# A linear-attention and dense-layer kernel: stores and loads of values issued from ScalarE's queue

## The chip, the cores and the metric

The kernel runs on one core of a Trainium2 chip. Times are device microseconds of that core for one execution. Five engines work side by side, each through its own list of instructions in order: TensorE (PE; its weight loads are shown as PEld), VectorE (DVE), ScalarE (ACT), GpSimd (POOL) and SyncE (SP). SP computes nothing; it issues transfers. A transfer (DMA) is issued by an instruction of one engine and then carried out by the core's 16 DMA engines; other engines learn through a semaphore that it has landed.

## The reference

The program computes gated linear attention and feeds its result to a dense layer. For each of 4 × 8 heads a 48 × 48 state decays row by row and takes in one key-value product per token; the output token is the query times the state:

```python
state = alpha[:, :, t, :, None] * state + np.einsum('bhd,bhe->bhde', k[:, :, t], v[:, :, t])
y[:, :, t] = np.einsum('bhd,bhde->bhe', q[:, :, t], state)
```

The 768 tokens of each of 4 batches, 384 wide, then go through two matrix products with a squared relu between them:

```python
h = x @ w_in                  # 3072 x 384 by 384 x 2048
r = np.maximum(h, 0.0)
g = r * r
return (g @ w_out)            # by 2048 x 384
```

Inputs and output are float32; the kernel multiplies in bfloat16.

## The kernel before

The work is cut into 12 units of 256 tokens (4 batches by 3 stretches of the sequence, batches running fastest). Each unit passes through these steps:

- Four loads bring alpha, k, q and v of the unit into one of four float32 buffers called raw (names lda, ldk, ldq, ldv with the unit's number; line 456). Unit g uses buffer g mod 4, so a load waits until unit g − 4 is done with that quarter of the buffer.
- The front turns alpha into logarithms (ACT), sums them over tokens with a triangular matrix (PE) and takes exponentials (ACT), which scale k and q (DVE) into a bfloat16 tile qks. v is cast to bfloat16 (vbf, names vc, mostly on POOL, L631).
- From unit 3 on, qks is transposed by DMA into kqt (names tr0 and tr1, L652), two transfers per unit issued by SP. Before that PE does it.
- The scores are multiplied on PE (psX and psZ, L838), masked on DVE (pm, L849), and with vbf and the carried state give the attention output in psX (L724 to L771), which ACT copies to xbf (names xe, L894).
- x is transposed to xt, from unit 4 on by a DMA that SP issues (L915), before that by PE (L909).
- The first layer (names s1, L965) makes 8 blocks per unit in two PSUM banks that alternate. Each block is relued into rr by ACT (re, L973) or DVE (L975) and squared into gt by ACT (sq, L987) or DVE (L983).
- The second layer (names s2, L1005) sums 16 products in psO for each half of the tokens; the result is copied to the output buffer osb by ACT (oe, L1012) or DVE (L1014), and for units 0 to 10 one store of 384 KB writes both halves to HBM (names out0_1 to out10_1, L1023). There are two buffers osb, so the evictions of unit g wait for the store of unit g − 2. The last unit has three smaller stores (L1016 and L943).

The loads of units 1 and 2 and the weights w_in and w_out are issued by POOL; all other transfers by SP.

The order in which each engine does its operations is written out by hand in a table of names, one list per engine (TABLES, L203). `schedule` takes the lists as they are; `place` then puts a semaphore wait ahead of an operation wherever something it needs runs on another engine or is a transfer and isn't known to be done through earlier waits of the same engine. Each engine works through its list in order, so an operation that waits holds back all that stand behind it.

What decides the engine for a transfer is the first argument of `add` in `load` (L458) and in `second_layer` (the call of `add` behind `store`, L1022), together with the list in which the name stands. A transfer's semaphore is named after what it moves and the engine that issues it.

Of the kernel before, what the change touches and what calls it, by code (L numbers as in the profile page):

```python
# [24 lines left out]
class Program:  # L25
# [13 lines left out]
    def add(self, eng, fn, cost, prio, reads=(), writes=(), name="", dma=None, lag=0, after=(), mode=("F", "F"),  # L39
            alts=None):  # L40

        reads, writes = ([h for k in keys for h in ((k + (0,), k + (1,)) if len(k) == self.HALVED.get(k[0]) else (k,))]
                         for keys in (reads, writes))
        choices = {eng: (fn, cost)}
        if alts:
            choices.update(alts)
        op = Op(choices, prio, name)
        op.idx = len(self.ops)
        op.lag = lag
        op.mode = mode  # L50
        if dma is not None:
            op.sem = (dma, 0)
        for o in after:
            op.deps[o] = True
        for k in reads:
            w = self.writer.get(k)
            if w is not None:
                op.deps[w] = True
            if k[0] == "ps":
                for r in self.readers.get(k, ()):  # L60
                    op.deps.setdefault(r, False)
        for k in writes:
            w = self.writer.get(k)
            if w is not None:
                op.deps[w] = True
            for r in self.readers.get(k, ()):
                if r is not op:
                    op.deps.setdefault(r, False)
        for k in reads:
            self.readers.setdefault(k, []).append(op)  # L70
        for k in writes:
            self.writer[k] = op
            self.readers[k] = []
        op.deps.pop(op, None)
        self.ops.append(op)
        return op
# [93 lines left out]
    def emit(self):  # L170
# [54 lines left out]
    "act": """  # L225
        table copycaus ln0_0 ln1_0 ei0_0 ea0_0 ei1_0 ea1_0 ec0_0 ec1_0 et00_0 et10_0 vc0 ln1 vc1 ei1 ea1 xe0 ec1 xv0
        re0_0 re0_1 sq0_1 re0_2 re0_3 ln2 xe1 ei2 ea2 re0_6 ec2 re0_7 es2 re1_0 re1_1 sq0_5 re1_3 et1_2 sq1_1 sq1_3
        oe0_0 ln3 ei3 ea3 re1_7 ec3 sq1_5 ln4 es3 re1_6 xe2 ei4 ea4 lm4 oe1_0 re2_1 ec4 re2_0 ln5 es4 re2_2 ei5
        re2_3 re2_4 lm5 ea5 ec5 re2_5 sq2_1 sq2_5 oe1_1 xe3 ln6 re2_6 sq2_7 sq2_6 es5 re3_1 re3_0 ei6 ea6 re3_3 ec6
        re3_2 oe2_0 re3_5 ln7 lm6 re3_4 sq3_5 xe4 re3_6 sq3_7 ei7 es6 ea7 oe3_0 re4_1 xe5 ec7 lm7 re4_2 sq4_3 re4_4  # L230
        re4_5 sq4_5 oe3_1 re4_7 ln8 es7 ei8 re5_2 oe4_0 lm8 re5_3 ea8 re5_4 re5_5 xe6 oe4_1 es8 re5_7 sq5_7 sq5_6
        re6_0 re6_1 re6_2 re6_3 re6_4 ln9 re6_5 xe7 ei9 ea9 lm9 oe5_1 sq6_5 es9 re6_6 re6_7 sq6_6 sq6_7 re7_0 re7_1
        sq7_1 re7_3 lm10 ln10 sq7_3 re7_4 ei10 ea10 re7_6 lm11 es10 sq7_6 sq7_7 ln11 re8_0 ei11 re8_2 vc10 ea11
        re8_4 xe9 re8_5 oe7_1 sq8_7 re9_1 re9_0 sq9_1 re9_3 re9_2 sq9_3 xe10 es11 oe8_1 re9_7 sq9_7 re10_1 re10_0
        sq10_1 re10_2 re10_5 sq10_3 sq10_5 re10_6 sq10_7 re11_1 re11_0 oe10_0 re11_3 re11_2 sq11_3 re11_4 re11_5
        oe10_1 re11_6 re11_7 oe11_0 oe11_10
    """,
    "dve": """
        zzero zlinc zlstr zident zcaus zcaus1 zones zown zlaf0 own0 zlaf1 own1 zqks0 zqks1 zqks2 zlab0 zlab1 ekm0_0
# [13 lines left out]
        vc4 bk5 pr7 vc5 vc6 vc7 pr8 vc8 pr9 vc9 pr10 pr11 vc11  # L253
    """,
    "sp": """
        lda0 ldk0 ldq0 ldv0 lda3 ldv3 ldk3 lda4 ldq3 ldq4 ldk4 lda5 ldv4 tr1_3 tr0_3 lda6 ldq5 tr1_4 ldk5 tr0_4
        out0_1 lda7 ldv5 ldk6 tr1_5 tr0_5 ldv6 xt4 out1_1 ldq6 ldk7 ldq7 ldv7 xt5 lda8 tr1_6 tr0_6 out2_1 ldk8 ldq8
        tr1_7 tr0_7 xt6 ldv8 lda9 out3_1 tr1_8 tr0_8 ldq9 xt7 ldv9 ldk9 lda10 out4_1 lda11 tr1_9 xt8 ldk10 ldq10
        out5_1 tr0_9 ldv10 ldv11 tr0_10 tr1_10 xt9 ldk11 ldq11 out6_1 out7_1 xt10 tr0_11 tr1_11 out8_1 xt11 out9_1
        out10_1 out11_0 out11_10 out11_11  # L260
    """,
}

# [1 line left out]
def pe_ns(count, cols, at_once=1):  # L265
    return count * max(cols / 2.4 + 2.5, 25) / at_once


def act_ns(n):
    return 180 + n * 0.8333  # L270


def dve_ns(n, rate=1.0):
    return 150 + n / 0.96 / rate
# [6 lines left out]
def bass_gla_recurrent__then__act_relu_squared_kernel(  # L281
# [25 lines left out]
    POOL_LOADS = (1, 2)  # L307
# [56 lines left out]
    add = pr.add  # L364
# [25 lines left out]
    for buf, key, val in ((LINC[:], "linc", 1.0), (LSTR[:], "lstr", 1.0), (IDENT[:], "ident", 0.0),  # L390
# [3 lines left out]
        name="slinc")  # L394
    add("pool", select(LSTR[:], ALU.is_gt, 0.0, 0, [[1, 128]], -1), 300, -1e6, reads=[("lstr",)], writes=[("lstr",)],
        name="slstr")
# [7 lines left out]
    for c, key in enumerate(("caus", "caus1")):  # L404
        add("pool", select(flat[c], ALU.is_ge, 0.0, 128 * c, [[-1, 2], [1, 2], [2, 64]], -2), 400, -1e6 + 7,
            reads=[(key,)], writes=[(key,)], name=f"s{key}")
    add("act", lambda e: e.activation(flat[1][0:64], flat[0][0:64], AF.Copy), 400, -1e6 + 8,
        reads=[("caus",), ("caus1",)], writes=[("caus1",)], name="copycaus")
# [6 lines left out]
    def piece(fj):  # L415
        return max(w for w, (at, n) in enumerate(PIECES) if at <= fj)
# [24 lines left out]
    def load(g):  # L441
        b, i = units[g]
        t0 = i * T
        p0 = g * P
        r, la, qs, kt, pm, vb, x2 = (g % n for n in (NRAW, 2, NQKS, NKQT, NPM, NV, 2))
        first, last = i == 0, i == NST - 1
        sr, sw = 2 * b + i % 2, 2 * b + (i + 1) % 2

        for j, t, nm in ((0, alpha, "a"), (1, k, "k"), (2, q, "q"), (3, v, "v")):
            src = t[b, :, t0:t0 + T, :].rearrange("h (p j) d -> p h (j d)", j=2)  # L450
            dst, key = RAW[r][:, j].rearrange("p h j d -> p h (j d)"), ("raw", r, j)
            gate = AFTER.get((g, nm), AFTER.get(g))
            parts = ((0, slice(0, 4)), (1, slice(4, 8))) if (g, nm) in HALF_LOADS else (("", slice(0, 8)),)
            for x, hs in parts:
                def run(e, dst=dst[:, hs], src=src[:, hs]):
                    return e.dma_start(dst, src)  # L456

                ring = "pool" if g in POOL_LOADS else "sp"  # L458
                load_op[g, nm] = add(ring, run, 930 if ring == "pool" else 600, L_PRIO[g] + j, writes=[key if x == "" else key + (x,)],
                                     name=f"ld{nm}{g}{x}", dma=f"{nm}{r}{x}", after=[load_op[gate]] if gate else [])  # L460

# [527 lines left out]
    def second_layer(g):  # L989
        b, i = units[g]  # L990
        gt = g % NGT
        p0 = DENSE.get(g, g * P + 20500)
        ob = g % NOSB
        for j in range(2):
            rows = slice(b * S + i * T + j, b * S + i * T + T, 2)
            if g == G - 1 and j == 1:
                last_tile(gt, rows, p0 + P)
                continue
            psS, keyS = (psX[:, 0, 0:DM], ("ps", "X", 0)) if (g, j) in IN_X else (psO[:, 0:DM], ("ps", "O"))
            for sg in range(4):  # L1000
                ps_ = p0 + P * 0.5 + 600 + (j * 4 + sg) * P * 0.5 / 8

                def s2(pe, sg=sg, j=j, psS=psS):
                    for fj in range(sg * FT // 4, (sg + 1) * FT // 4):
                        ins = pe.matmul(psS, GT[gt][:, fj, j, :], WOUT[:, fj, :],  # L1005
                                        start=(fj == 0), stop=(fj == FT - 1))
                    return ins

                add("pe", s2, pe_ns(FT // 4, DM), ps_,
                    reads=[("gt", gt, fj) for fj in range(sg * FT // 4, (sg + 1) * FT // 4)] + [("wout", piece(sg * FT // 4))],  # L1010
                    writes=[keyS], name=f"s2_{g}_{j}_{sg}")
            add("act", lambda e, j=j, psS=psS: e.activation(OSB[ob][:, j], psS, AF.Copy), act_ns(DM), ps_ + 700,  # L1012
                reads=[keyS], writes=[("osb", ob, j)], name=f"oe{g}_{j}",
                alts={"dve": (lambda e, j=j, psS=psS: e.tensor_copy(OSB[ob][:, j], psS), dve_ns(DM))})  # L1014
            if g == G - 1:
                add("sp", lambda e, rows=rows: e.dma_start(out[rows, :], OSB[ob][:, 0]), 600, ps_ + 1300,  # L1016
                    reads=[("osb", ob, 0)], name=f"out{g}_0", dma=f"o{ob}", lag=600)
            elif j == 1:

                dst = out[b * S + i * T:b * S + i * T + T, :].rearrange("(p j) n -> p (j n)", j=2)  # L1020

                def store(e, dst=dst):  # L1022
                    return e.dma_start(dst, OSB[ob][:].rearrange("p j n -> p (j n)"))  # L1023

                add("sp", store, 600, ps_ + 1300, reads=[("osb", ob, 0), ("osb", ob, 1)], name=f"out{g}_1",
                    dma=f"o{ob}")

    L_PRIO = {g: (g - 4) * P for g in range(G)}
# [3 lines left out]
    for g in range(3, G):  # L1032
        ORDER += [f"f{g}", f"w{g - 1}", f"p{g}"]
    ORDER += [f"y{G - 1}"]
    AFTER = {1: (0, "a"), ("win", 0): (0, "k"), ("win", 1): (0, "k"), 2: ("win", 0), ("wout", 0): ("win", 1),
             ("wout", 1): (2, "k"), 3: ("wout", 0)}
    load(0)
    load(1)
    for w in range(len(PIECES)):
        weight(0, w)  # L1040
    load(2)
    for w in range(len(PIECES)):
        weight(1, w)
    for st in ORDER:
        kind, g = st[0], int(st[1:])
# [46 lines left out]
```

## Time and profile before

| what | value |
|---|---|
| median of 3 timed runs | 176.03 us (175.4 to 178.41) |
| profiled execution | 174.4 us |
| its span, first to last instruction | 172.7 us |
| PE busy | 167.6 us, 97% of the span |
| PEld, DVE, ACT, POOL busy | 130.4, 122.3, 113.7, 26.9 us |
| queue of SP's transfers | 69024 packets, 26.75 MB, 66.6% of the 16 engines' time |
| queue of POOL's transfers | 1984 packets, 6.29 MB, 15.3% |

All of these but the timed runs come from one execution that was recorded by the hardware profiler. Issuing a transfer isn't counted as busy time; such rows are shown as SPq, with the time that the issuing instruction took, not the transfer itself. In a timeline row stand the start in us from the span's start, the duration in us, engine, line, operation, output and input, the count of instructions merged, and in brackets how long the engine was idle before and what ended that. In the chain of work that ended last, a row gives start, duration, engine, output and line. In the list of waits a row gives the engine and the line that waited, what it waited for, the total in us, how many times and the longest.

### The profile page before, as it was taken

How to read it: one execution, taken by the hardware profiler on the slowest of the kernel's cores; microseconds unless marked ns; L12 is line 12 of the kernel's file. 1: busy time of each engine (PE TensorE's matmuls, PEld its weight loads, DVE VectorE, ACT ScalarE, POOL GpSimd, SP SyncE). 2: the span in 40 equal slices, each digit the busy share in tenths (PEclk: the TensorE clock that was granted, in tenths of full speed). 3: DMA queues.
4: the chain of work that ended last, by engine and by line, in shares of the span. 5: the costliest groups of instructions: out<-in, count | busy, mean ns of one | idle time of the engine just before them, and what ended most of it. 6: DMA issues, size and time to landing. Idle time of an engine off the chain costs nothing.

```text
span 172.7 us, 5090 instructions
## 1 busy us (share of the span) xinstructions
PE 167.6 (97%) x2232; PEld 130.4 (76%) x2234; DVE 122.3 (71%) x202; ACT 113.7 (66%) x201; POOL 26.9 (16%) x37
## 2 busy tenths in 40 slices
PE   7999999899999999999999999999999999999994
PEld 2656888577887877888777878887787977778773
DVE  5379599679967979999796839679768663762110
ACT  4757768659789974588466589767552946356740
POOL 4920750030120040105000401220010000000000
PEclk9999999999999999999999999999999999999999
DMA  5999999999999998999995979949949448022022
GB/s 145 351 292 212 270 233 172 283 286 297 204 213 191 232 257 168 273 243 188 255 165 128 285 149 245 270 90 286 277 66 238 174 77 181 4 53 87 0 93 91
DMA packets 71030, 33.36 MB, mean 193 GB/s; under 512 B 67552, under 2 KB 67808, under 8 KB 71008
## 3 DMA queue, kind: packets, MB, share of 16 engines
q1 hardware_dynamic: 69024, 26.75, 66.6%
q0 software_dynamic: 1984, 6.29, 15.3%
q8 instruction: 17, 0.28, 0.6%
q14 instruction: 5, 0.04, 0.1%
HBM read 25.17 MB, written 4.72 MB: 173 GB/s over the span
## 4 chain that ended last, share of the span: by engine, by line
PE 79%; DMA 16%; POOL 3%; issue 1%; DVE 0%
PE psO L1005 34%; PE psWH L965 33%; DMA wout<-in_moe_w_out_dram 5%; DMA win<-in_moe_w_in_dram 5%; DMA raw<-in_k_dram 3%; POOL raw L456 3%; PE psX L735 2%; PE psZ L703 2%; DMA raw<-in_alpha_dram 2%; PE psX L838 2%; PE psX L724 2%; PE psX L935 2%; PE psZ L838 1%; PE psWH L574 1%; PE psX L909 0%
## 5 line engine op out<-in xcount | busy, mean ns | idle before, releaser
L965 PE MATMUL psWH<-xt,win 128*128 128x256 bf16 x576 | 73.0, 274 | 0.0
L1005 PE MATMUL psO<-wout,gt 128*128 128x384 bf16 x368 | 68.2, 326 | 0.6 <-DMA wout<-in_moe_w_out_dram 0.6
L965 PEld LDWEIGHTS psWH<-xt,win 128*128 128x128 bf16 x576 | 65.2, 145 | 4.6 <-ACT xt L923 0.4
L973 ACT ACTIVATE rr<-psWH 128x512 bf16<-128x512 f32 x70 | 41.3, 595 | 21.9 <-PE psWH L965 20.8
L1005 PEld LDWEIGHTS psO<-wout,gt 128*128 128x128 bf16 x368 | 35.0, 98 | 19.0 <-DMA wout<-in_moe_w_out_dram 0.8
L987 ACT ACTIVATE gt<-rr 128x1024 bf16<-128x1024 bf16 (+1 forms) x31 | 26.9, 890 | 3.5 <-DVE rr L975 3.1
L975 DVE TENSOR_SCALAR rr<-psWH 128x512 bf16<-128x512 f32 x26 | 17.7, 688 | 10.0 <-PE psWH L965 9.7
L983 DVE TENSOR_TENSOR gt<-rr 128x1024 bf16<-128x1024 bf16 (+1 forms) x29 | 17.2, 597 | 9.6 <-ACT rr L973 9.4
L631 POOL CAST vbf<-raw 128x768 bf16<-128x768 f32 x9 | 8.1, 899 | 68.3 <-DMA raw<-in_v_dram 68.3
L849 DVE TENSOR_TENSOR pm<-psX,caus 128x1024 bf16<-128x1024 f32 x12 | 14.6, 1220 | 4.0 <-PE psZ L838 4.0
L849 DVE TENSOR_TENSOR pm<-psZ,caus 128x1024 bf16<-128x1024 f32 x12 | 14.6, 1219 | 3.4 <-PE psZ L838 3.4
L1012 ACT ACTIVATE osb<-psO 128x384 f32<-128x384 f32 x14 | 6.9, 491 | 10.1 <-PE psO L1005 8.8
L1061 PE MATMUL psO<-zero 128*128 128x512 bf16 (+1 forms) x32 | 9.9, 437 | 1.5 <-DVE zero L376 1.3
L894 ACT ACTIVATE xbf<-psX 128x768 bf16<-128x768 f32 x10 | 8.1, 808 | 4.5 <-PE psX L724 4.1
L636 DVE TENSOR_TENSOR qks<-raw,eq 128x384 bf16<-128x384 f32 x18 | 10.5, 587 | 0.4 <-ACT eq L611 0.3
L641 DVE TENSOR_TENSOR qks<-raw,ek 128x768 bf16<-128x768 f32 x11 | 10.5, 954 | 0.1
L585 ACT ACTIVATE ek<-psWH 128x384 f32<-128x384 f32 x10 | 4.9, 489 | 5.9 <-PE psWH L574 3.8
L567 POOL TENSOR_TENSOR prd<-raw 128x384 f32<-128x384 f32 x6 | 6.2, 1035 | 16.3 <-DMA raw<-in_alpha_dram 16.3
L1014 DVE COPY osb<-psO 128x384 f32<-128x384 f32 x9 | 5.0, 555 | 4.8 <-PE psO L1005 4.6
L594 DVE TENSOR_TENSOR ek<-ek,raw 128x384 f32<-128x384 f32 x9 | 5.0, 553 | 3.7 <-ACT ek L585 3.7
L568 ACT ACTIVATE lab<-prd 128x384 bf16<-128x384 f32 x10 | 5.2, 518 | 2.4 <-POOL prd L567 1.4
L1061 PEld LDWEIGHTS psO<-zero 128*128 128x128 bf16 x34 | 3.2, 109 | 4.5 <-issue 1.9
(116 smaller groups left out, 166.0 us busy)
## 6 DMA issues: line engine op xcount, KB each, us to landing
out_dram<-osb SPq DMA_DIRECT2D x11, 384.0 KB, 4.4
raw<-in_alpha_dram SPq DMA_DIRECT2D x10, 384.0 KB, 5.0
raw<-in_k_dram SPq DMA_DIRECT2D x10, 384.0 KB, 4.2
raw<-in_q_dram SPq DMA_DIRECT2D x10, 384.0 KB, 5.0
raw<-in_v_dram SPq DMA_DIRECT2D x10, 384.0 KB, 5.1
win<-in_moe_w_in_dram POOLq DMA_DIRECT2D x2, 768.0 KB, 10.3
wout<-in_moe_w_out_dram POOLq DMA_DIRECT2D x2, 768.0 KB, 8.6
raw<-in_alpha_dram POOLq DMA_DIRECT2D x2, 384.0 KB, 4.6
```

The lines of the kernel that those rows point to most:

```text
L631: add("pool", lambda e: e.tensor_copy(vout, vin), 830, p0 + 900, reads=[("raw", r, 3)], writes=[("vbf", vb)], name=f"vc{g}", alts={"act": ...
L636: add("dve", lambda e, j=j, dst=dst: e.tensor_tensor(dst, RAW[r][:, 2, :, j, :].rearrange("p (n x) d -> p n x d", x=2), EQ[la][:, j].rearr ...
L641: add("dve", lambda e, a=a, E=E: e.tensor_tensor(QKS[qs][:, a, :, :, 0:D], RAW[r][:, 1 + a].rearrange("p h j d -> p j h d"), E[la][:].rear ...
L849: add("dve", lambda e, hf=hf, psT=psT: e.tensor_tensor(PM[pm][:, hf].rearrange("p r n j t -> p (r n) (j t)"), psT[:, :, :].rearrange("p r ...
L894: add("act", lambda e: e.activation(XBF[x2][:], psX[:, :, 0:HD], AF.Copy), act_ns(2 * HD), p0 + 6100, reads=[("ps", "X", 0), ("ps", "X", 1 ...
L965: ins = pe.matmul(psH[hb][:, i * T:(i + 1) * T], WIN[:, kk, hidden(fj)], mov, start=(kk == 0), stop=(kk == KT - 1))
L973: add("act", lambda e, hb=hb, rr=rr: e.activation(rr, psH[hb], AF.Relu), act_ns(512), pu + 600, reads=[("ps", "H", hb)], writes=[("rr", rb ...
L975: alts={"dve": (lambda e, hb=hb, rr=rr: e.tensor_scalar(rr, psH[hb], 0.0, None, ALU.max), dve_ns(512))})
L983: add("dve", lambda e, dst=dst, sq=sq: e.tensor_tensor(dst, sq, sq, ALU.mult), 148 + k * 267, pu + 1200, reads=[("rr", rb, h) for h in ran ...
L987: "act": (lambda e, dst=dst, sq=sq: e.activation(dst, sq, AF.Square), act_ns(k * 512))})
L1005: ins = pe.matmul(psS, GT[gt][:, fj, j, :], WOUT[:, fj, :], start=(fj == 0), stop=(fj == FT - 1))
L1061: pr.schedule(TABLES, (zero, lambda n: lambda pe: pe.matmul(psO[:, 0:n], ZERO[:, 0:128], ZERO[:, 0:n], skip_group_check=True)))
```

## The change

The stores of units 0 to 10 and the loads of v of units 4 to 11, 19 transfers in all, are issued from ACT's list instead of SP's. In ACT's list each name is put between the operations beside which SP issued it; the order of all other names is as before, on every engine.

```diff
@@ ACT's list: names put in (the rest unchanged)
+ldv4 after ln4      out0_1 after re2_6    ldv5 after sq2_6
+ldv6 after sq3_5    out1_1 after sq3_7    ldv7 after ea7
+out2_1 after re4_7  ldv8 after es8        out3_1 after sq5_7
+ldv9 after lm9      out4_1 after es9      out5_1 after ea10
+ldv10 after sq7_6   ldv11 after re8_0     out6_1 after oe7_1
+out7_1 after sq8_7  out8_1 after sq9_7    out9_1 after re10_6
+out10_1 after oe10_1
@@ SP's list: the same 19 names taken out
@@ in load(g)
-                ring = "pool" if g in POOL_LOADS else "sp"
+                ring = "pool" if g in POOL_LOADS else "act" if nm in "v" and g >= 4 else "sp"
@@ in second_layer(g)
-                add("sp", store, 600, ps_ + 1300, reads=[("osb", ob, 0), ("osb", ob, 1)], name=f"out{g}_1",
+                add("act", store, 600, ps_ + 1300, reads=[("osb", ob, 0), ("osb", ob, 1)], name=f"out{g}_1",
                     dma=f"o{ob}")
```

The evictions that wait for a store (L1012 on ACT, L1014 on DVE) and the casts of v (L631) now wait on the semaphores of ACT's transfers. In ACT's list the stores of units 7 and 10 carry a wait for an eviction on ACT itself and the store of unit 9 one for an eviction on DVE; the other 16 moved transfers carry no wait of their own there. SP's end waits for the last stores of both engines.

More of the change, by code (lines that the diff above doesn't have):

```diff
@@ L227 @@
         re0_0 re0_1 sq0_1 re0_2 re0_3 ln2 xe1 ei2 ea2 re0_6 ec2 re0_7 es2 re1_0 re1_1 sq0_5 re1_3 et1_2 sq1_1 sq1_3
[L228 to L236, printed above, removed]
+        oe0_0 ln3 ei3 ea3 re1_7 ec3 sq1_5 ln4 ldv4 es3 re1_6 xe2 ei4 ea4 lm4 oe1_0 re2_1 ec4 re2_0 ln5 es4 re2_2 ei5
+        re2_3 re2_4 lm5 ea5 ec5 re2_5 sq2_1 sq2_5 oe1_1 xe3 ln6 re2_6 out0_1 sq2_7 sq2_6 ldv5 es5 re3_1 re3_0 ei6
+        ea6 re3_3 ec6 re3_2 oe2_0 re3_5 ln7 lm6 re3_4 sq3_5 ldv6 xe4 re3_6 sq3_7 out1_1 ei7 es6 ea7 ldv7 oe3_0 re4_1
+        xe5 ec7 lm7 re4_2 sq4_3 re4_4 re4_5 sq4_5 oe3_1 re4_7 out2_1 ln8 es7 ei8 re5_2 oe4_0 lm8 re5_3 ea8 re5_4
+        re5_5 xe6 oe4_1 es8 ldv8 re5_7 sq5_7 out3_1 sq5_6 re6_0 re6_1 re6_2 re6_3 re6_4 ln9 re6_5 xe7 ei9 ea9 lm9
+        ldv9 oe5_1 sq6_5 es9 out4_1 re6_6 re6_7 sq6_6 sq6_7 re7_0 re7_1 sq7_1 re7_3 lm10 ln10 sq7_3 re7_4 ei10 ea10
+        out5_1 re7_6 lm11 es10 sq7_6 ldv10 sq7_7 ln11 re8_0 ldv11 ei11 re8_2 vc10 ea11 re8_4 xe9 re8_5 oe7_1 out6_1
+        sq8_7 out7_1 re9_1 re9_0 sq9_1 re9_3 re9_2 sq9_3 xe10 es11 oe8_1 re9_7 sq9_7 out8_1 re10_1 re10_0 sq10_1
+        re10_2 re10_5 sq10_3 sq10_5 re10_6 out9_1 sq10_7 re11_1 re11_0 oe10_0 re11_3 re11_2 sq11_3 re11_4 re11_5
+        oe10_1 out10_1 re11_6 re11_7 oe11_0 oe11_10
     """,
@@ L255 @@
     "sp": """
[L256 to L260, printed above, removed]
+        lda0 ldk0 ldq0 ldv0 lda3 ldv3 ldk3 lda4 ldq3 ldq4 ldk4 lda5 tr1_3 tr0_3 lda6 ldq5 tr1_4 ldk5 tr0_4 lda7 ldk6
+        tr1_5 tr0_5 xt4 ldq6 ldk7 ldq7 xt5 lda8 tr1_6 tr0_6 ldk8 ldq8 tr1_7 tr0_7 xt6 lda9 tr1_8 tr0_8 ldq9 xt7 ldk9
+        lda10 lda11 tr1_9 xt8 ldk10 ldq10 tr0_9 tr0_10 tr1_10 xt9 ldk11 ldq11 xt10 tr0_11 tr1_11 xt11 out11_0
+        out11_10 out11_11
     """,
```

## The prediction

> **What bounds the kernel now.** I read the page's shares first, then the busy time by stretch, then who waits for whom from 33.2 us to the end, and last the timelines of SP, ScalarE (ACT) and the chain.
>
> ```profile
> PE 167.6 (97%) x2232; PEld 130.4 (76%) x2234; DVE 122.3 (71%) x202; ACT 113.7 (66%) x201; POOL 26.9 (16%) x37
> 33.22:54.60 21.38, 21.38 (x305) 16.50 (x306) 17.94 (x31) 16.10 (x33) 3.48 (x4) 1.00 1.05 243
> 54.60:80.00 25.40, 25.40 (x369) 20.30 (x367) 22.53 (x35) 18.77 (x36) 4.20 (x4) 1.00 1.06 235
> 80.00:105.00 25.00, 25.00 (x375) 19.80 (x372) 18.63 (x29) 16.05 (x30) 2.94 (x3) 1.00 0.88 187
> 105.00:130.00 25.00, 25.00 (x317) 20.32 (x314) 19.42 (x29) 17.08 (x31) 3.67 (x4) 1.00 0.92 211
> 130.00:155.00 25.00, 24.93 (x334) 19.81 (x332) 16.20 (x25) 13.68 (x20) 0.00 (x0) 1.00 0.48 119
> PE psO L1005 <- DMA wout<-in_moe_w_out_dram: 0.6, 1, 0.6
> ACT rr L973 <- PE psWH L965: 19.5, 28, 1.6
> ACT osb L1012 <- PE psO L1005: 8.8, 7, 2.2
> ```
>
> A stretch's row gives its length, then busy time of PE, PEld, DVE, ACT and POOL; the last three numbers are granted clock, DMA share and GB/s. Over the five stretches from 33.22 to 155 us PE is busy 121.71 of 121.78 us, at clock 1.00. After 33.2 us the only wait that PE shows is 0.6 us for a weight load. So TensorE sets the end, and no transfer that SP issues is late for it: what SP is relieved of buys at most 0.07 us in these stretches. ACT works 81.7 of the same 121.78 us, and its largest idle times end with a PE result (19.5 and 8.8 us). That idle time is the cover under which ACT can take new work. The question is only whether it lies where the new work is put.
>
> **What is moved and what it costs.** The first moved transfer stands behind the logarithm of unit 4, at 40 us; the head up to 33.22 us is untouched. Nineteen DMA issues go to ACT: 11 stores and 8 loads of values. Each stands in ACT's order where ACT was when SP issued it. The same bytes start within about a microsecond of where they started, and the 26 transposes and the loads of alpha, k and q on SP stand where they stood, with gaps closed up.
>
> The price of one issue on ACT is on no row. The nearest rows are the same instructions on SP:
>
> ```profile
> 40.46 1.16 SPq L456 DMA_DIRECT2D raw<-in_v_dram  x1
> 52.81 2.41 SPq L652 DMA_TRANSPOSE kqt<-qks  x1
> 55.27 0.57 SPq L1023 DMA_DIRECT2D out_dram<-osb  x1
> 55.89 0.43 SPq L456 DMA_DIRECT2D raw<-in_alpha_dram  x1
> 56.37 1.52 SPq L456 DMA_DIRECT2D raw<-in_v_dram  x1
> 57.93 1.52 SPq L456 DMA_DIRECT2D raw<-in_k_dram  x1
> 68.27 0.57 SPq L1023 DMA_DIRECT2D out_dram<-osb  x1
> 92.07 0.58 SPq L456 DMA_DIRECT2D raw<-in_v_dram  x1
> 94.49 3.75 SPq L652 DMA_TRANSPOSE kqt<-qks  x2
> 118.51 2.76 SPq L456 DMA_DIRECT2D raw<-in_v_dram  x2
> L1023 SPq DMA_DIRECT2D out_dram<-osb x11: 333/1124/1327, 55.3 to 164.4; - x11
> ```
>
> Two groups show. The first issues after a pause take 0.43 to 0.58 us; from the third in a row on they take 1.1 to 1.5 us, as if the queue were full and each had to wait for room (my reading; 384 KB in 1.5 us is 256 GB/s, the rate at which the engines run there). ACT's queue gets at most two issues close together, so I take 0.57 us each. The bounds are 0 (ACT's sequencer issues while an earlier ACTIVATE still runs) and 1.5 us.
>
> Nineteen times 0.57 is 10.8 us of ACT. What reaches PE is, place by place, the issue less its cover: ACT's next idle time, plus the margin between ACT's result and the PE work that needs it.
>
> ```profile
> 41.41 0.81 ACT L894 ACTIVATE xbf<-psX 128x768 bf16<-128x768 f32 x1
> 43.04 0.34 PE psX L909 x6
> 57.22 1.25 ACT L973 ACTIVATE rr<-psWH 128x512 bf16<-128x512 f32 x2 [0.19 <-PE psWH L965]
> 58.48 1.31 PE psWH L965 x12
> 66.17 0.81 ACT L894 ACTIVATE xbf<-psX 128x768 bf16<-128x768 f32 x1 [1.31 <-PE psX L724]
> 69.84 0.49 ACT L585 ACTIVATE ek<-psWH 128x384 f32<-128x384 f32 x1 [1.10 <-PE psWH L577]
> 71.57 0.49 ACT L1012 ACTIVATE osb<-psO 128x384 f32<-128x384 f32 x1 [0.44 <-DMA out_dram<-osb]
> 71.96 0.59 ACT L973 ACTIVATE rr<-psWH 128x512 bf16<-128x512 f32 x1
> 73.49 1.46 PE psWH L965 x12
> 95.30 1.25 ACT L973 ACTIVATE rr<-psWH 128x512 bf16<-128x512 f32 x2 [1.25 <-PE psWH L965]
> 103.86 0.49 ACT L1012 ACTIVATE osb<-psO 128x384 f32<-128x384 f32 x1 [0.73 <-PE psO L1005]
> 117.05 0.60 ACT L973 ACTIVATE rr<-psWH 128x512 bf16<-128x512 f32 x1 [0.94 <-PE psWH L965]
> 121.77 0.49 ACT L585 ACTIVATE ek<-psWH 128x384 f32<-128x384 f32 x1 [1.37 <-PE psWH L574]
> 131.70 0.63 ACT L987 ACTIVATE gt<-rr 128x512 bf16<-128x512 bf16 x1 [2.34 <-DVE rr L975]
> 163.84 0.49 ACT L1012 ACTIVATE osb<-psO 128x384 f32<-128x384 f32 x1 [0.70 <-PE psO L1005]
> 164.49 1.25 ACT L973 ACTIVATE rr<-psWH 128x512 bf16<-128x512 f32 x2 [0.16 <-PE psWH L965]
> 165.11 2.60 PE psO L1005 x16
> L983 DVE TENSOR_TENSOR gt<-rr 128x1024 bf16<-128x1024 bf16 (+1 forms) x29 | 17.2, 597 | 9.6 <-ACT rr L973 9.4
> ```
>
> - Load of v4 at 40.6 us: the activation behind it that PE needs first ends at 42.22 us and PE's transpose of it starts at 43.04 us, a cover of 0.82 us. Loss 0.
> - Store 0 and load v5, both between 55.5 and 56.6 us, only two squares apart: together 1.14 us. ACT then idles 0.19 us, its next relu ends near 57.82 us (half of the pair of 1.25 us) and PE needs that at 58.48 us: cover 0.19 + 0.66 = 0.85 us. **Loss 0.29 us**, the one place where the plain price does not fit.
> - Load v6 (1.31 us idle behind it), store 1 (1.10 us), load v7 (0.44 us idle, then a relu that ends at 72.55 for PE at 73.49 us: 1.38 us), load v8 with store 3 (1.14 us against 1.25), load v9 (0.73 us), store 5 (0.94 us), loads v10 and v11 (1.14 us against 1.37), stores 6 and 7 (0.57 us against 2.34, and a second idle time behind): no loss. For stores 2, 4, 8 and 9 I quote no row and assume the same.
> - Stores 7, 9 and 10 wait for an eviction. Only store 10 waits for the ACT operation just ahead of it: that ends at 164.33 us, the two relus queued behind the store start at 164.49 us, so they are 0.57 − 0.16 = 0.41 us late. They end at 165.74 us, a square on DVE takes 0.6 us, and PE needs it for the last quarter of the 16 products that start at 165.11 us, at 167.06 us: cover 0.72 us. Loss 0.
>
> One further term. ACT's eviction at 71.57 us waits for store 1 to free its buffer:
>
> ```profile
> DMA to landing us min/median/max: 2.6/4.4/5.9
> ACT osb L1012 <- DMA out_dram<-osb: 1.1, 2, 0.7
> ```
>
> Store 1 was issued at 68.27 us, so it landed after some 3.3 us. On its own queue it shares the engines with the k and q loads that SP issues behind it, instead of being ahead of them. At the median of 4.4 us the eviction starts 1.2 us later; the relu behind it has 0.94 us: loss 0.3 us. Bounds: 0 gained (PE is not waiting for it), 5.9 − 3.3 − 0.94 = 1.7 us lost.
>
> **Sum:** 0.29 + 0.3 = 0.6 us. The profiled execution took 174.4 us (span 172.7), so 175.0 us on its own scale. The median of the three timed runs shown is 176.03 us, 1.63 above it; on that scale 176.6 us, which I predict. Those three runs spread from 175.4 to 178.41, so about 2% (3.5 us) is what a measurement of this kernel tells from no change.
>
> **Rivals.**
>
> *The issues take as long on ACT as the slow group on SP* (1.15 us each). For it: DMA share is 1.05 and 1.06 between 33 and 80 us, so room is short for any queue. Against it: the quick issues of 0.57 and 0.43 us at 55.27 and 55.89 us lie in that same stretch. Price: v4 0.33, store 0 with v5 2.3 − 0.85 = 1.45, v8 with store 3 2.3 − 1.25 − 0.66 (the margin of a relu as at 58 us) = 0.4, v9 0.42 carried into store 4, 1.57 less a cover like 0.85 = 0.7, store 10 1.15 − 0.16 − 0.72 = 0.3: 3.2 us, so 177.6 on the profile's scale and 179.2 on the median's, just inside 2%.
>
> *Slower: an issue on ACT has to wait for the issue that SP is in.* Place: wherever SP is at a transpose (2.41 us at 52.81, two in 3.75 us at 94.49) or at a slow load. With the moved issues gone, SP enters the next instruction sooner, right where ACT issues. Worst price: store 0 and v5 meet loads of 0.43 and 1.52 us, 1.14 + 1.95 − 0.85 = 2.2; store 3 meets a transpose of 1.9, 1.14 + 0.6 (the load before it) + 1.9 − 1.25 − 0.66 = 1.7; v10 and v11 meet one of 1.9, 1.14 + 1.9 − 1.37 − 0.66 = 1.0; store 5 one of 1.9, 0.57 + 1.9 − 0.94 − 0.66 = 0.9. That is 5.8 us at worst. With each wait halved the same four places cost 1.3 + 0.5 + 0.1 + 0 = 1.9. I take 4, nearly midway: 178.4, on the median's scale 180.0 (+2.3%); at worst 181.8. It decides once an issue on ACT takes over about 1.2 us on average. In the trace only SP uses this kind of queue, so no row speaks for or against. The Trainium skill, "Perfetto Trace Analysis", section "DMA Instruction — HWDGE (DVE, Sync)", describes the descriptor generator as a block that issuing sequencers share, locked for one instruction at a time, with the wait for the lock inside the recorded duration. By that rule this rival would be the forecast; no run here shows it yet.
>
> *Faster: SP was short of time.* SP's rows stand end to end around 55 and 92 us, and it would now send transposes a microsecond or so earlier. But PE has 0.07 us of idle time to give back up to 155 us, and the tail's stores stay on SP. It gives 174.3 on the profile's scale, 175.9 on the median's. The skill's section "DMA Optimizations" on that page advises to balance issues over engines where the issuing one is full; by it the move should help, and the rows of PE say that here it cannot show.
>
> That the change is not made can be left out: ACT's order gains 19 DMA instructions.
>
> **How the numbers follow.** Forecast (0 to 1.5 us lost) 0.45; slow issues 0.22, a third of it beyond 2%; meeting SP 0.26, nearly all beyond 2%; SP relieved 0.05, of which a gain over 2% is at most 0.02, since PE bars it; anything else 0.02. So faster 0.02, same 0.63, slower 0.35. The range must hold the forecast, the slow issues and most of the meeting with SP, and a run as quick as the quickest shown: 175.0 to 182.0 us.
>
> **What the profile after would show.** Right: DMA rows on ACT of 0.4 to 0.7 us, PE busy nearly without a break from 33.2 us, at most 1 us of PE waits on ACT, most near 58 and 73 us. Slow issues: rows on ACT of 1.1 us and more, wherever they lie. Meeting SP: the long ones only where SP is at a transpose at the same time, and new PE waits for relus near 58, 95 and 120 us. The prediction is wrong if ACT stands still for longer than its issue rows, or if the transposes land later behind the mixed queues, so that PE waits for transposed keys or x, which it does not now.

## The result and the profile after

The changed kernel took 181.7 us (median, 180.31 to 181.85) against 176.13 us before in the same comparison: a ratio of 1.0313, 95% interval 1.0243 to 1.0384. It is slower. Its profiled execution took 181.85 us, span 180.1 us, against 174.4 and 172.7 us.

The shares of the page, the waits of PE from 33 us on, and the busy time by stretch of the changed kernel:

```profile
PE 169.7 (94%) x2234; PEld 131.4 (73%) x2234; DVE 124.6 (69%) x202; ACT 113.9 (63%) x201; POOL 27.5 (15%) x37
```

```profile
PE psX L838 <- DMA kqt<-qks: 3.9, 2, 2.2
PE psWH L965 <- DVE tmp L811: 0.4, 1, 0.4
```

```profile
33.22:54.60 21.38, 21.38 (x286) 16.25 (x284) 18.57 (x31) 16.81 (x33) 4.16 (x4) 1.00 0.97 238
54.60:80.00 25.40, 25.40 (x417) 20.23 (x415) 22.14 (x37) 19.36 (x36) 2.87 (x4) 1.00 1.11 224
80.00:105.00 25.00, 22.87 (x297) 18.20 (x296) 18.93 (x27) 14.31 (x27) 3.61 (x4) 1.00 0.93 187
105.00:130.00 25.00, 23.01 (x295) 18.21 (x285) 17.58 (x27) 17.36 (x32) 2.84 (x3) 1.00 0.92 207
```

ACT's busy time is what it was (113.9 against 113.7 us) and no relu is late. PE now waits in two places for kqt, the transposed keys and queries, which it never did before; with the third wait it is idle for 2.1 us between 80 and 105 us and for 2.0 us between 105 and 130 us. The row with "DVE tmp" has to be read twice: the block that waits takes in xt and win, not tmp. The transpose of x for unit 6 landed at 99.24 us, 0.14 us before the block started; in four other kernels with this wait the block starts 0.13 to 0.14 us after that landing too, and there the row names the transpose.

ACT's timeline in the changed kernel shows what an issue costs there:

```profile
56.43 0.81 ACT L894 ACTIVATE xbf<-psX 128x768 bf16<-128x768 f32 x1
56.63 0.36 ACTq L1023 DMA_DIRECT2D out_dram<-osb  x1
57.14 0.51 ACT L568 ACTIVATE lab<-prd 128x384 bf16<-128x384 f32 x1
82.78 0.60 ACT L973 ACTIVATE rr<-psWH 128x512 bf16<-128x512 f32 x1 [0.54 <-PE psWH L965]
82.78 0.37 ACTq L1023 DMA_DIRECT2D out_dram<-osb  x1
```

The issue (0.36 us) lies inside the running ACTIVATE, and the next ACTIVATE starts as if it weren't there. All 19 take 0.34 to 0.44 us, and the 14 of them that overlap an issue of SP's own are no longer than the others (0.34 to 0.41 us).

How late the transposes land: SP's timeline row for the two transposes of unit 6, with the time from issue to landing of the same two instructions, first before, then after:

```profile
77.52 3.24 SPq L652 DMA_TRANSPOSE kqt<-qks  x2
DMA to landing us min/median/max: 3.9/4.9/5.9
```

```profile
80.09 3.36 SPq L652 DMA_TRANSPOSE kqt<-qks  x2
DMA to landing us min/median/max: 4.0/5.9/7.8
89.20 0.42 PE L838 MATMUL psX<-kqt 64*64 64x128 bf16 x16 [1.73 <-DMA kqt<-qks]
```

Issued in the same time (3.36 against 3.24 us), the later of the two lands after 7.8 us instead of 5.9. The scores of unit 6 wait 1.73 us for it. For tr0 of unit 9, before and after:

```profile
DMA to landing us min/median/max: 5.5/5.5/5.5
```

```profile
DMA to landing us min/median/max: 9.5/9.5/9.5
```

There the issue itself is longer, too: 3.55 us on SP instead of 1.47.

To place the loss I split each trace at the first score matmul of each unit (L838) and at the last tile's second layer, and subtract the stretches of before. The stretches from unit 7 to 8 and from 11 to that last second layer change by under 0.05 us and are left out:

| kernel | ahead of unit 3 | 3 to 5 | 5 to 6 | 6 to 7 | 8 to 9 | 9 to 10 | 10 to 11 | from unit 3 on |
|---|---|---|---|---|---|---|---|---|
| changed | +2.57 | 0.0 | 1.80 | 0.60 | 2.22 | 0.0 | 0.18 | **4.81** |
| changed, once more | +0.93 | 0.1 | 1.81 | 0.69 | 3.10 | 1.67 | 0.62 | 8.00 |
| stores alone | +1.47 | 0.0 | 1.65 | 0.0 | 0.84 | 0.81 | 0.60 | 3.91 |
| loads alone | −0.36 | 0.0 | 0.0 | 0.89 | 1.36 | 0.0 | 0.0 | 2.28 |
| tiny loads on ACT | +1.17 | 0.0 | 0.34 | 0.0 | 0.49 | 0.0 | 0.0 | 0.85 |
| six back on SP | +1.04 | 0.0 | 0.0 | 0.0 | 0.0 | 0.0 | 0.0 | 0.01 |
| six alone on ACT | +1.19 | 0.0 | 1.62 | 0.75 | 2.53 | 1.62 | 0.64 | 7.17 |
| all 19, six retimed | +0.08 | 0.0 | 0.0 | 0.0 | 0.0 | 0.0 | 0.0 | 0.00 |
| one queue, three ahead | +0.69 | 0.0 | 0.0 | 0.0 | 2.54 | 1.61 | 0.0 | 4.15 |
| store 2 alone on ACT | +0.89 | 0.0 | 0.66 | 0.0 | 0.0 | 0.0 | 0.0 | 0.68 |
| unit 9 back on SP | +1.34 | 0.7 | 1.64 | 1.20 | 0.0 | 0.0 | 0.64 | 4.18 |
| one queue, load 10 ahead | +2.81 | 0.0 | 0.0 | 0.0 | 0.80 | 0.0 | 0.0 | 0.80 |
| one queue, store 2 between | +0.80 | 1.0 | 0.10 | 0.0 | 0.04 | 0.0 | 0.0 | 1.12 |

The first column follows no edit. The kernels are alike up to 40 us, and from there to the scores of unit 3 only the load of v of unit 4 differs; the column ranges from −0.36 to +2.57 us where that load is on ACT and from +0.69 to +2.81 where it is on SP. It comes out anew in each execution (below). From unit 3 on the changed kernel loses 4.81 us, in three places: scores of unit 6, first layer of unit 6, scores of unit 9. Three of its four runs have a mean granted clock of 0.991, and so have three of four with six alone on ACT; the latter count as slow, so that kernel has no ratio.

### The profile page after: what moved, and what is told of

Read it like the earlier page. It is cut to its first block, busy times and chain, and to the rows that moved or that the text cites. A ratio compares the mean times of both kernels' runs of the same rounds, so it can differ in the third digit from the quotient of the medians.

```text
span 180.1 us, 5091 instructions
## 1 busy us (share of the span) xinstructions
PE 169.7 (94%) x2234; PEld 131.4 (73%) x2234; DVE 124.6 (69%) x202; ACT 113.9 (63%) x201; POOL 27.5 (15%) x37
## 4 chain that ended last, share of the span: by engine, by line
PE 64%; DMA 23%; DVE 5%; POOL 3%; SPq 2%; issue 1%; ACT 0%
PE psWH L965 27%; PE psO L1005 24%; DMA kqt<-qks 13%; DMA raw<-in_alpha_dram 5%; DMA win<-in_moe_w_in_dram 5%; POOL raw L456 2%; PE psX L838 2%; PE psX L735 2%; PE psZ L703 2%; DVE rr L975 2%; PE psX L724 2%; PE psX L935 1%; SPq L652 1%; PE psZ L838 1%; PE psWH L574 1%; DVE qks L636 1%
## 5 line engine op out<-in xcount | busy, mean ns | idle before, releaser
L965 PE MATMUL psWH<-xt,win 128*128 128x256 bf16 x576 | 74.3, 277 | 0.4 <-DVE tmp L811 0.4
L631 POOL CAST vbf<-raw 128x768 bf16<-128x768 f32 x9 | 8.3, 920 | 68.1 <-DMA raw<-in_v_dram 68.1
L1012 ACT ACTIVATE osb<-psO 128x384 f32<-128x384 f32 x14 | 6.9, 491 | 10.0 <-PE psO L1005 8.0
L641 DVE TENSOR_TENSOR qks<-raw,ek 128x768 bf16<-128x768 f32 x11 | 11.1, 1009 | 0.8 <-DMA raw<-in_k_dram 0.8
L838 PE MATMUL psX<-kqt 64*64 64x128 bf16 x192 | 5.0, 222 | 4.0 <-DMA kqt<-qks 3.9
L838 PEld LDWEIGHTS psX<-kqt 64*64 64x64 bf16 x192 | 3.1, 106 | 6.9 <-DMA kqt<-qks 4.9
L1014 DVE COPY osb<-psO 128x384 f32<-128x384 f32 x9 | 5.0, 552 | 4.0 <-PE psO L1005 3.9
```

The lines of the kernel that those rows point to most:

```text
L631: add("pool", lambda e: e.tensor_copy(vout, vin), 830, p0 + 900, reads=[("raw", r, 3)], writes=[("vbf", vb)], name=f"vc{g}", alts={"act": ...
L641: add("dve", lambda e, a=a, E=E: e.tensor_tensor(QKS[qs][:, a, :, :, 0:D], RAW[r][:, 1 + a].rearrange("p h j d -> p j h d"), E[la][:].rear ...
L838: ins = pe.matmul(psT[64 * c:64 * c + 64, rr_, o:o + 128], keys, mov)
L965: ins = pe.matmul(psH[hb][:, i * T:(i + 1) * T], WIN[:, kk, hidden(fj)], mov, start=(kk == 0), stop=(kk == KT - 1))
```

## The experiments

Theory A: ACT's issues are free; its transfers delay transposes that SP issued. Theory B: the issues hold up ACT. Theory C: the loss lies in the head. Later came D (a second queue slows transposes wherever its transfers lie) and E (a long wait costs PE clock). The diffs are shortened to the lines that carry the edit, some written out more plainly than in the kernel; what stands behind # or in < > describes lines that are left out.

**Stores alone.**

```diff
-ring = "pool" if g in POOL_LOADS else "act" if nm in "v" and g >= 4 else "sp"
+ring = "pool" if g in POOL_LOADS else "sp"        # ldv4 to ldv11 back in SP's list
```

> The 11 stores alone on ACT; all loads on SP as before. Theory A (a transpose that SP has issued shares the DMA engines with transfers that ACT issues after it, and lands late; the issue on ACT is free): the stores of units 2 and 5 still meet the transposes of units 6 and 9, so the scores of unit 6 come about 1.7 us late and those of unit 9 about 1 us, x of unit 6 hardly: 178.5 to 179.5 us. Theory B (issues hold up ACT): 11 of 19 parts of the loss, spread over the whole run with no wait for kqt: about 179.4 us. Theory C (most of the loss lies in the first 33 us, in work that the change does not touch): the head is as long as in the changed kernel or as in the one before, whichever the run draws, not in step with the stores.

179.97 us, ratio 1.020 (1.0107 to 1.0293). The scores of unit 6 come 1.65 us late, those of unit 9 0.84, and x of unit 6 is on time: A in these places. Two losses behind unit 9 were not foreseen: 0.8 us up to unit 10, of which 0.6 us is a wait for an eviction on DVE, and 0.6 us up to the scores of unit 11, where PE waits 0.53 us for kqt (the third of the waits in the first row below): tr1 of unit 11 lands 5.9 us after its issue instead of 4.1, beside store 8.

```profile
PE psX L838 <- DMA kqt<-qks: 2.9, 3, 1.6
PE psO L1005 <- DVE osb L1014: 0.6, 1, 0.6
```

**Loads alone.**

```diff
-add("act", store, 600, ps_ + 1300, ...
+add("sp", store, 600, ps_ + 1300, ...             # out0_1 to out10_1 back in SP's list
```

> The 8 loads of values alone on ACT; all stores on SP as before. Theory A: the loads of units 8 and of 10 and 11 still meet the transposes of x of unit 6 and of unit 9; the scores of unit 6 are on time, x of unit 6 about 0.7 us late, the scores of unit 9 1 to 1.5 us: 177.5 to 178.5 us. Theory B: 8 of 19 parts of the loss, about 178.5 us, with no wait for kqt. Theory C: as for the stores alone.

177.62 us, ratio 1.0072 (1.0037 to 1.0108). Unit 6's scores are on time, its x 0.9 us late, unit 9's scores 1.36 us late, as A has it. The two halves together lose more (6.2 us) than the whole change in its first profile (4.8), but not at unit 9, where they add up to it (0.84 + 1.36 against 2.22): the excess comes mainly from the two losses of the stores behind unit 9, and 0.3 us of it from x of unit 6.

**Issues without their bytes.**

```diff
+TINY = nc.alloc_sbuf_tensor("tiny", [128, 152], FP32)
+for x, n in enumerate(<the 19 places in ACT's list>):
+    add("act", lambda e, x=x: e.dma_start(TINY[:, 8 * x:8 * x + 8], moe_w_in[0:128, 0:8]), 600, 0, name=f"tiny_{n}", dma="y")
```

> The kernel before, all its transfers on SP; at each of the 19 places ACT issues a load of 4 KB (128 rows of 32 bytes, into a tile that nothing reads) in place of the 384 KB. Theory A: the issues cost nothing, 176.1 us within 0.5%, and ACT's busy time and PE's lack of waits are as before. Theory B: most of the loss is there, 179 to 182 us. Theory C: the first 33 us are as long as in the changed kernel in some runs, whatever stands behind.

175.69 us, ratio 1.003 (0.9989 to 1.0072). B falls: nineteen issues on ACT at the same places, 18 of them 0.33 to 0.45 us long and one of 1.02, and no loss that can be told from none. ACT's rows are as in the changed kernel:

```profile
56.63 0.63 ACT L990 ACTIVATE gt<-rr 128x512 bf16<-128x512 bf16 x1
56.78 0.34 ACTq L1065 DMA_DIRECT2D tiny<-in_moe_w_in_dram  x1
57.15 0.63 ACT L990 ACTIVATE gt<-rr 128x512 bf16<-128x512 bf16 x1
```

Even 4 KB on the second queue put 0.34 and 0.49 us before the scores of units 6 and 9, in this one profile.

**The six that lie beside a needed transpose, back on SP.**

```diff
+ACT_V, ACT_S = (4, 5, 6, 7, 9), (0, 1, 3, 4, 6, 7, 9, 10)   # ldv8, 10, 11 and out2, 5, 8 in SP's list as before
```

> The change, but the six transfers that lie beside a transpose whose landing PE awaits (stores 2, 5 and 8, loads of values 8, 10 and 11) are back on SP at their old places; the other 13 stay on ACT. Theory A: the waits near the scores of units 6 and 9 and the first layer of unit 6 are gone, 176 to 177 us. Theory B: 13 of 19 parts of the loss stay, about 180 us. Theory C: between 176 and 178 us by the head alone.

175.72 us, ratio 0.9999 (0.9962 to 1.0035). Thirteen transfers on ACT cost nothing that can be measured, and PE's list of waits has only the weight load again:

```profile
PE psO L1005 <- DMA wout<-in_moe_w_out_dram: 0.6, 1, 0.6
```

**The complement, those six alone on ACT.**

```diff
+ACT_V, ACT_S = (8, 10, 11), (2, 5, 8)
```

> The complement: stores 2, 5 and 8 and loads of values 8, 10 and 11 alone on ACT, the other 13 back on SP. Theory A: the whole loss between the scores of unit 3 and the last block stays (4.8 us in the changed kernel, 4 to 5 here), 180 to 181 us, with PE waiting for kqt at the scores of units 6 and 9. Theory B: 6 of 19 parts, about 177.7 us.

183.3 us (179.83 to 183.6): the loss is all there, and more than expected, 7.2 us in the profile instead of 4 to 5. Of the excess 1.6 us lies between units 9 and 10, where PE's blocks run slowly. That led to theory E.

**All 19 on ACT, the six at other places.**

```diff
 (ACT's list)
+out2_1 after oe3_0   ldv8 after re5_3   out5_1 after re7_0
+ldv10 after sq7_1    ldv11 after ea11   out8_1 after sq10_1
```

> All 19 on ACT as in the change, but these six at other places of ACT's list, where the transposes under way have microseconds to spare: store 2 after the eviction of unit 3's first half, load 8 after relu 3 of unit 5, store 5 after relu 0 and load 10 after square 1 of unit 7, load 11 after the exponential ea of unit 11, store 8 after square 1 of unit 10. Theory A: no waits for kqt, 176 to 177 us. Theory B, and a theory D (a second queue slows transposes by being there at all, wherever its transfers lie): 180 to 182 us as in the changed kernel.

176.33 us, ratio 1.004 (0.9986 to 1.0093), none of the waits for kqt or x left, 0.00 us from unit 3 on. So neither the number of transfers on ACT nor the second queue as such costs; B and D fall. What counts is which transpose is under way when ACT's transfer comes. One that was left beside ACT's transfers shows it without costing anything: tr0 of unit 4, beside store 0, lands after 7.3 us instead of 5.9 and uses up all but 0.27 of the 1.64 us that it had to spare.

**One queue, transposes put behind transfers.**

```diff
 (before, SP's list)
-lda8 tr1_6 tr0_6 out2_1 ...  out5_1 tr0_9 ldv10 ldv11
+lda8 out2_1 tr1_6 tr0_6 ...  out5_1 ldv10 ldv11 tr0_9
```

> The kernel before, all on SP's one queue, but transposes put behind transfers that stood after them: store 2 ahead of the two transposes of unit 6, loads 10 and 11 ahead of the transpose tr0 of unit 9. If the loss in the changed kernel is the lost place in the line (each transfer of 384 KB takes about 1.2 us of the engines), the scores of unit 6 come 0.5 to 1.3 us late and those of unit 9 about 2 us: 178 to 179.5 us. If sharing with a second queue is what costs, this loses under 1 us: 176 to 177 us.

179.75 us, ratio 1.0234 (1.0155 to 1.0312). At unit 6 nothing is lost, a miss: the store had landed at 81.55 us, and tr0 at 85.07 us, in time for the scores at 85.52. At unit 9 two loads ahead cost 2.54 us. PE's timeline there, and the busy time and clock in three stretches of 3.41 us:

```profile
126.20 0.64 PE L839 MATMUL psX<-kqt 64*64 64x128 bf16 x16 [2.47 <-DMA kqt<-qks]
127.20 2.65 PE L1006 MATMUL psO<-wout,gt 128*128 128x384 bf16 x8
```

```profile
122.81:126.22 3.41, 0.94 (x13) 0.70 (x11) 0.74 (x2) 1.85 (x4) 0.82 (x1) 1.00 1.16 146
126.22:129.63 3.41, 3.41 (x40) 2.02 (x41) 2.30 (x3) 0.00 (x0) 0.00 (x0) 0.50 0.69 103
129.63:133.04 3.41, 3.41 (x75) 2.77 (x74) 1.21 (x3) 1.39 (x2) 0.00 (x0) 1.00 0.02 5
```

After 2.47 us of idle time PE runs at half its clock for 3.41 us. Eight products that take 1.47 us in the kernel before take 2.65, and 1.61 us more are lost by unit 10. Of the 4.15 us in all, 2.54 are lost place and 1.61 clock.

**Store 2 alone on ACT.**

```diff
+ACT_V, ACT_S = (), (2,)
```

> Only the store of unit 2 on ACT, 18 transfers on SP as before. Theory A: one wait of PE for kqt, of 1.5 to 2 us, at the scores of unit 6, and nothing else: 177.6 to 178 us. Theory B: within 0.3 us of before.

176.17 us, ratio 1.0023 (0.9973 to 1.0073). One wait for kqt, at unit 6, as A says, but 0.66 us, not 1.5 to 2. The six-alone kernel is the same program up to there and lost 1.62 in its profile, so the size differs from execution to execution; the time alone would not have shown it.

**The changed kernel once more.**

> The changed kernel itself, once more. From the scores of unit 3 to the last block it was 4.8 us longer than before, and a further 2.6 us of its profiled run lay ahead of the scores of unit 3. Theory A: the 4.8 us come again within 1 us, from the same three places; what lies ahead of the scores of unit 3 is drawn anew in each run, as in the kernel before. Theory C: the 2.6 us ahead come again as well. Theory E (a wait of PE of 2.2 us or more near the scores of unit 9 also costs clock): runs with a granted clock near 0.99 are more frequent here than in the kernel before.

183.56 us, ratio 1.0404 (1.0332 to 1.0476). The three places come again (1.81, 0.69, 3.10), the head does not (0.93): C falls. The size does not come again: 8.0 us instead of 4.8 within 1, a miss of A's. The wait at unit 9 is now 3.03 us, and the clock drops behind it, which adds 1.67 us; the scores of unit 11 lose 0.6, as with the stores alone. The wait at unit 9, and three stretches: around the 1.74 us of waiting at unit 6, around the wait at unit 9, and behind that one:

```profile
129.61 0.42 PE L838 MATMUL psX<-kqt 64*64 64x128 bf16 x16 [3.03 <-DMA kqt<-qks]
85.81:89.22 3.41, 1.67 (x42) 1.47 (x42) 0.87 (x1) 1.07 (x4) 0.00 (x0) 1.00 1.16 227
126.77:130.18 3.41, 0.57 (x32) 0.48 (x33) 2.69 (x5) 1.18 (x2) 0.00 (x0) 1.00 1.34 265
130.18:133.59 3.41, 3.41 (x21) 1.85 (x14) 2.95 (x3) 0.48 (x2) 0.82 (x1) 0.50 0.84 127
```

All four of its runs have a mean clock of 0.982 to 0.991. That number doesn't say where a run was slow: in the changed kernel's first profile, with 0.991, it was the head.

**Store 5 and loads 10 and 11 back on SP.**

```diff
+ACT_V, ACT_S = (4, 5, 6, 7, 8, 9), (0, 1, 2, 3, 4, 6, 7, 8, 9, 10)
```

> The change with store 5 and loads of values 10 and 11 back on SP, 16 transfers on ACT. Theory A: the wait at the scores of unit 9 is gone, those at the scores of unit 6 and at x of unit 6 stay: 2.4 to 2.7 us over before between the scores of unit 3 and the last block, 178 to 179 us. Theory E: hardly any run with a clock of 0.99. Theory B: 16 of 19 parts of the loss, about 180.8 us.

179.2 us, ratio 1.0157 (1.0089 to 1.0226). The wait at unit 9 is gone, and no run has a clock under 1.0, as E has it. In the profile 4.18 us are lost, not 2.4 to 2.7: x of unit 6 costs 1.2, the scores of unit 11 0.6 (beside store 8), and the scores of unit 4 0.7. For the last, the profile names nothing that PE waited for, but tr0 of unit 4, beside store 0 and load 5 on ACT, landed 0.09 us before the scores. Its time to landing, before and here:

```profile
DMA to landing us min/median/max: 5.9/5.9/5.9
```

```profile
DMA to landing us min/median/max: 7.7/7.7/7.7
```

So this is most likely the same lateness, at a place that had 1.64 us to spare.

**One queue, one load ahead.**

```diff
 (before, SP's list)
-out5_1 tr0_9 ldv10 ldv11
+out5_1 ldv10 tr0_9 ldv11
```

> One queue, as in the kernel before, with only load 10 put ahead of the transpose tr0 of unit 9 (it was loads 10 and 11, and store 2 ahead of unit 6). The lost place: the scores of unit 9 come about 1.2 us late instead of 2.5. Theory E: a wait that short does not bring the clock down, so nothing follows, 177 to 177.5 us; if the slower clock that followed there had another cause, 1.6 us come on top, about 178.8 us.

176.88 us, ratio 1.0043 (0.9999 to 1.0087). Unit 9 is 0.80 us late (1.2 expected), and nothing follows between units 9 and 10 (0.0 us): the short wait costs no clock, as E says.

**One queue, the store between the two transposes.**

```diff
 (before, SP's list)
-tr1_6 tr0_6 out2_1
+tr1_6 out2_1 tr0_6
```

> One queue, as in the kernel before; store 2 is put between the two transposes of unit 6, so that it stands directly ahead of the transpose tr0 for which PE has no margin. If a lost place of one store is all that the second queue costs there, tr0 lands about 1.2 us later and the scores of unit 6 start 1.1 to 1.3 us late, less than the 1.6 to 1.8 us with the store on ACT's queue among others (0.7 us with that store alone there). If a store on a queue of its own costs the transpose more than a store ahead of it, the loss here stays well under 1.2 us. 176.5 to 177.5 us.

177.44 us, ratio 1.0134 (1.0028 to 1.024), but of the 1.12 us in the profile 0.97 lie ahead of the place that is changed, between units 3 and 5, where PE waits 0.32 and 0.39 us for results of DVE; why is open, so the ratio says little about the edit. At unit 6 the store ahead costs 0.10 us, not 1.1 to 1.3. The landings, worked out from the trace's semaphore events and counted from the issue of tr1:

| kernel | tr1 of unit 6 | tr0 of unit 6 | store 2 |
|---|---|---|---|
| before (tr1 tr0 store) | 3.9 | 7.2 | 8.0 |
| store between | 3.7 | 7.4 | 6.4 |
| store 2 alone on ACT | 3.9 | 7.9 | 8.4 |
| changed | 4.0 | 9.1 | 8.9 |
| changed, once more | 4.2 | 8.7 | 8.1 |

So at unit 6 a store ahead in the same queue costs the transpose 0.1 us, and the same store on a second queue 0.7 to 1.8. The lost place in the line is not the whole mechanism there.

## Why the prediction was right, and where it was not

The time lay in the range (175.0 to 182.0), but the forecast itself, 176.6 us and most likely no change, was 5 us too low. That the range held 181.7 was luck: it reached that far for a rival whose mechanism did not happen, and "slower" (0.35) had most of its chance from there, too.

- **PE bounds the kernel, nothing can be gained:** right. With SP relieved of 13 or 19 issues and no needed transpose held up, the time is that of before (0.9999 and 1.004).
- **The price of an issue, 0.57 us, and its covers:** too high, and harmless. The rows are 0.34 to 0.44 us and lie under the running ACTIVATE, so even the one loss that I worked out (0.29 us at 58 us) is not there: 0.0 from unit 3 to 5. My lower bound of 0 was the value. (384 KB in 1.5 us is 262 GB/s, not 256; nothing hangs on it.)
- **Store 1 lands later (0.3 us):** wrong. It was issued at 70.54 us and landed at 73.87, after 3.3 us against 3.2 before. The eviction that does wait longer is unit 4's, for store 2, 1.59 us, and PE is already waiting for the transpose at that time.
- **Store 10:** right, no loss (0.00 us from the scores of unit 11 to the last second layer, 0.03 to the end of the span).
- **The step that failed** is "the 26 transposes and the loads of alpha, k and q on SP stand where they stood", read as if they would land when they did. The transposes do stand there, but they land later. The runs showed in its place up to 4 us: tr0 of unit 9 lands 9.5 us after its issue instead of 5.5. The trace of before had the warning, which I did not read because PE showed no wait: tr0 of unit 6 landed at 84.75 us and the scores start at 84.83, a margin of 0.08 us; tr0 of unit 9 had 0.5 (122.45 to 122.97), x of unit 6 0.9 (93.57 to 94.44). "No wait" was read as "not late"; it said nothing on how nearly late. I named this as a way for the prediction to be wrong and gave it no price and no chance.
- **Rival, slow issues on ACT:** did not happen.
- **Rival, ACT waits for SP's issue:** its time (180.0 us) came closest, its mechanism did not happen. ACT's issue at 82.78 us takes 0.37 us while SP is in its two transposes from 80.09 to 83.45 us. The Trainium skill, "Perfetto Trace Analysis", section "DMA Instruction — HWDGE (DVE, Sync)", has the descriptor generator locked for one instruction at a time; between SP and ACT these rows show no such wait, nor do the other 13 that overlap an issue of SP's.

Why at unit 6 a transfer on the second queue holds back a transpose more than one ahead of it in the same queue was not settled; at unit 9 two loads ahead cost as much (2.54 us) as the change (2.22). The Trainium skill, "DMA: Bandwidth & Descriptors", section "Queues, rings and completion order", says that each DMA engine takes turns between the queues, a packet at a time; by that rule a transfer that comes later on the other queue gets turns while a transpose is still under way, which fits the late landings. It does not by itself give the difference between 0.1 and 0.7 to 1.8 us at unit 6. What would tell it apart, transposes alone against one steady stream on the other queue, was not run.

## What to carry to other kernels

Before moving transfers to a second queue, find for each transfer that stays when it lands and when it is needed, and mind those with little to spare: here transposes with 0.08 to 1.18 us in hand came too late, most likely one with 1.64 as well, and one landed 4 us later than before. While all stood in one queue, the bulk transfers behind an urgent one did not do this to it; from a second queue they did. If a second queue is wanted, place its transfers where the urgent ones have slack; here that made the same 19 transfers cost nothing. An issue on ACT cost nothing here; it is the bytes that must be scheduled.

## What was not expected of the hardware

Waits of PE of 2.47 us (one queue, three ahead), 3.03 us (the changed kernel once more) and 2.46 us (six alone) were each followed by 3.41 us at half the clock, worth 1.6 to 1.7 us, which is about half of 3.41. The wait of 2.2 us in the changed kernel's first profile was not, though it differs by only 0.3 us. In the traces' records of the clock it changes, once PE is at work, only at points that lie a multiple of 3.41 us apart within one execution (as 126.22 and 129.63 us above). As far as these runs go, what tells the cases apart is how much PE worked in the 3.41 us ahead of such a point: 0.57, 0.94 and 0.95 us ahead of these drops, 1.67 us ahead of none (at unit 6, above). The 2.2 us lie across two such stretches, and in each PE still worked 2.28 us or more:

```profile
125.63:129.04 3.41, 2.38 (x19) 1.80 (x17) 1.47 (x3) 1.09 (x2) 0.00 (x0) 1.00 1.24 184
129.04:132.45 3.41, 2.28 (x44) 1.72 (x45) 2.81 (x5) 1.22 (x2) 0.75 (x1) 1.00 1.21 216
```

So a transfer a few tenths of a microsecond later can cost 2 us, and whether it does depends on where the wait falls. E is right in that a long wait can cost clock, and too simple in going by its length alone. The Trainium skill, "TensorE: Matmul & The Clock Gate", section "Part 1: The HAM clock gate", puts the return to half rate after an idle window of about 3.4 us; the halved rate and the length agree with the rows of 0.50, while here 2.47 us of idle time, in a stretch in which PE worked 0.94 us, sufficed.

The head, too, differs from execution to execution: alpha of unit 2, issued by POOL, landed 4.6 us after its issue in the profile of before and 6.1 us after it in the changed kernel's, on the same instructions. There PE waited 2.0 us for what follows from alpha, worked 1.42 us of 3.41, and then ran at half the clock:

```profile
23.24:26.65 3.41, 1.42 (x48) 1.20 (x43) 2.39 (x4) 1.37 (x3) 2.92 (x3) 1.00 1.00 198
26.65:30.06 3.41, 3.41 (x21) 2.68 (x19) 1.98 (x3) 2.19 (x6) 0.08 (x1) 0.50 0.90 146
```

This may be why the kernel before spreads from 174.3 to 179.6 us; only one of its executions was profiled, so that is not shown. Where less than 1% was in question, stretches of the traces were therefore compared here rather than whole times.
